# An attention kernel's eight-score phase: one exponential each for the first two scores, and a table of three phases for the PSUM banks

## The chip, the cores and the metric

The kernel runs on one core of one Trainium2 chip. The metric is the device time of one execution in microseconds (us). Beside the times there is a profile of one execution, in which the engines are called PE (TensorE, the matmuls), PEld (TensorE's loads of the stationary operand, called weight loads), ACT (ScalarE), DVE (VectorE), POOL (GpSimd) and SP (the engine that issues most DMAs). L829 means line 829 of the kernel.

## The reference

The output mixes two branches by a gate for each token: 32-head softmax attention, and an MLP over the token axis. All arrays are float32.

```python
x = A_x                                        # (1, 2048, 512)
g = sigmoid((x * gate_w).sum(-1, keepdims=True))
# a: full attention, H = 32 heads of Dh = 16, S = 2048 tokens
q, k, v = split_heads(x @ wqkv)
p = softmax(einsum("bhqd,bhkd->bhqk", q, k) * Dh ** -0.5)
a = merge_heads(einsum("bhqk,bhkd->bhqd", p, v)) @ wo
# b: token-mixing MLP, F = 1792
h = layernorm(x)
u = gelu(einsum("bsd,sf->bdf", h, w1) + b1)
b = transpose(einsum("bdf,fs->bds", u, w2) + b2)
out = g * a + (1 - g) * b
```

## The kernel before, in words

The kernel first makes v, then q and k (split in a high and a low float32r part and written to DRAM), then the first layer of the MLP. From about 305 us on it runs the attention, with the MLP's second layer and the output projection laid beside it on TensorE. The change lies in that part alone.

**Groups and phases.** There are 32 groups (`grp`): a pair of heads by half of the queries. A group has 8 phases, so there are 256 phases in all. A phase makes eight scores, s0 to s7 here: each is one matmul of 64 rows of contraction, 128 keys by 512 queries, written to a PSUM bank of its own (`score`, L829). The other 64 rows of the array are given to a matmul of the dense work (`dn`, L895), which is issued right behind a score and runs beside it. Most phases have six dense matmuls: then s0 and s1 run beside each other, on the two halves of the rows, and s2 to s7 have a dense one each. In the phases with eight dense matmuls every score has one. The table of the dense work (`put`, L672, with its sizes at L694, L696, L700, L706 and L707) gives eight to the first pair of phases, to nine pairs in the second layer's tiles 4, 8 and 12 and to the last eight pairs, that is to 36 of the 256 phases.

**Banks.** Of PSUM's eight banks one (`dn`) belongs to the dense work, and seven form `banks` (RING = 7). The table `TURN` says for each phase, in turn, which banks the eight scores take, and which bank v's products take. It has four rows, and four more that mirror them, so it repeats after eight phases.

**Exponentials.** ScalarE reads the scores and writes the exponentials into a tile `pt` with room for two scores. `exponentials` (L844) issues one instruction for two banks that lie side by side (128x1024) as soon as both scores are issued. In three of four rows a phase has four such instructions, called e0 to e3 here. In the third row the last two scores lie in banks 6 and 0, and e3 is two instructions of one bank each (128x512), which share one `pt`. The pool `ptp` has six buffers (L539), so e2 of a phase writes into the buffer that e0 of the phase before has filled.

**v's products.** After the scores of a phase TensorE multiplies v with the exponentials of the phase before (`apply_v`, L775, its matmul at L789). In the trace that is 32 matmul records in each phase, in four pairs of scores: the first pair reads s0 and s1 of the phase before, and so releases e0's `pt`. The products go to one bank, `av_bank`, and VectorE adds them to the group's sum (L809).

**What sets the order.** The order of each engine's instructions is written out by hand (`tc.manual_schedule`). TensorE's in one phase is: s0 to s7 with the dense matmuls, then v's products. `reads` and `writes` put a wait for each use of a bank: a score waits for what last read its bank.

In a phase two uses of banks come around within the phase itself: s7 takes a bank that s0 or s1 had, and v's products take the other of the two (row one: `3, 4, 5, 6, 0, 1, 2, 3`, v's products in 4). The other scores take banks from the phase before: s4 and s5 those of its e3, s6 the one that its v's products had and VectorE has read.

The POOL `token` (L899) orders the two halves of the dense rows, which add to one bank from phase to phase. `slow` holds VectorE's larger steps (reciprocals of the softmax sums, the scaling and splitting of attention output that `fetch_o` has brought from DRAM, L607 to L620), at most one for each phase, put ahead of the phase's addition.

Of the kernel before, what the change touches and what calls it, by code (L numbers as in the profile page):

```python
# [10 lines left out]
F32 = mybir.dt.float32  # L11
# [3 lines left out]
AF = mybir.ActivationFunctionType  # L15
# [7 lines left out]
P = 128  # L23
# [8 lines left out]
NB = 512  # L32
NQ = S // NB
VC = DH + 1
SCALE = DH**-0.5
# [24 lines left out]
def gated_mix(ctx: ExitStack, tc: tile.TileContext, a_x, a_wqkv, a_wo, b_w1, b_b1, b_w2, b_b2, gate_w, out):  # L60
    nc = tc.nc
# [353 lines left out]
    with tc.tile_pool(name="ln1", bufs=3, side="right") as ln, tc.tile_pool(name="gl", bufs=2, side="right") as gl:  # L415
# [22 lines left out]
        beside = {mybir.EngineType.Activation, mybir.EngineType.DVE, mybir.EngineType.Pool}  # L438
# [6 lines left out]
        for f0, cs in order.items():  # L445
            n = min(NB, F - f0) // P
# [65 lines left out]
    def second_out(t, ps):  # L512
# [13 lines left out]


    TURN = [
# [4 lines left out]
    ]  # L533
    TURN += [(tuple(RING - 1 - s for s in scores), RING - 1 - b) for scores, b in TURN]

    o_d = [[dram.tile([P, QW], F32, name=f"o{h}{k}") for k in range(ND)] for h in range(2)]
    r_d = [[dram.tile([P // DH, QW], F32, name=f"r{h}{k}") for k in range(ND)] for h in range(2)]
# [183 lines left out]
    def reads(ins, *at):  # L721
        for before in recent:
            if before.ins.engine != ins.ins.engine:
                tc.declare_no_dep(ins.ins, before.ins, reason="another bank")
        recent.append(ins)
        for bank in at:
            readers[bank].append(ins)
            for mm in writers[bank].values():
                tc.add_manual_dep(ins.ins, mm.ins.name, SYNC, reason="the bank is written")
# [45 lines left out]
    def apply_v(late, bank, end=False):  # L775

        if not late:
            return
        g, units = late
        pairs = [sorted(units[n : n + 2], key=lambda u: u[2]) for n in range(0, N_S, 2)]  # L780
        av = banks[:, bank, :]
        taken = [0, 0]

        for pair in pairs:
            for i, c, qb, pt, act in pair:
                taken[qb] += 1
                for h in range(2):
                    j = 2 * qb + h
                    mm = nc.tensor.matmul(  # L789
                        av[32 * j : 32 * j + VC, i * QC : (i + 1) * QC],  # L790
                        v[:, c, g % NP * 2 + i, :],
                        pt[:, h * QC : (h + 1) * QC],
                        start=taken[qb] == 1,
                        stop=taken[qb] == len(pairs),
                    )
                    writes(mm, bank, j, act)

        there = {(i, qb) for i, _, qb, *_ in units}
        if len(there) == 4:
            parts = list(zip(column_halves(sums[g]), column_halves(av))) if end else [(sums[g], av)]  # L800
        else:
            parts = []
            for i in sorted(range(2), key=lambda i: -sum(k[0] == i for k in there)):
                qbs = [qb for qb in range(2) if (i, qb) in there]
                if qbs:
                    at = slice(64 * qbs[0], 64 * (qbs[-1] + 1)), slice(i * QC, (i + 1) * QC)
                    parts.append((sums[g][at], av[at]))
        for x, y in parts:
            reads(nc.vector.tensor_tensor(x, y, x, ALU.add), bank)  # L809

    engines = {getattr(mybir.EngineType, name) for name in ("PE", "Activation", "DVE", "Pool", "SP")}
    with tc.manual_schedule(engines=engines):
        kt, qt = {0: load_k(0)}, {0: load_q(0)}
        late, fence = None, None

        for n, (step, *args) in enumerate(first):
            if n and n % 12 == 0:
                split_weight(nc.vector.tensor_copy, nc.vector.tensor_tensor)
            ps, a, b, start, stop, done = step(*args)
            nc.tensor.matmul(ps, a, b, start=start, stop=stop)  # L820
            if done:
                done()

        def score(grp, i, n, turn, units):

            c, qb = n // 2, (n + i) % 2
            bank = turn[len(units)]
            rows = slice(i * HALF, i * HALF + ROWS)
            mm = nc.tensor.matmul(  # L829
                banks[:, bank, :],  # L830
                kt[grp][rows, c * P : (c + 1) * P],
                qt[grp][rows, qb * NB : (qb + 1) * NB],
                start=True,
                stop=True,
            )
            writes(mm, bank)
            units.append([i, c, qb, None, None])
            beside = [m for m, unit in enumerate(units) if unit[3] is None and abs(turn[m] - bank) == 1]
            if beside:
                exponentials(turn, units, [sorted((beside[0], len(units) - 1), key=lambda m: turn[m])])  # L840
            elif len(units) == N_S:
                exponentials(turn, units, [[m] for m, unit in enumerate(units) if unit[3] is None])

        def exponentials(turn, units, runs):  # L844
            pt = ptp.tile([P, 2, NB], F32, name="pt")
            n = 0
            for run in runs:
                at = [turn[m] for m in run]
                dst = pt[:, n : n + len(at), :]
                act = nc.scalar.activation(dst, banks[:, at[0] : at[-1] + 1, :], AF.Exp, scale=SCALE)  # L850
                reads(act, *at)
                for m in run:
                    units[m][3:] = pt[:, n, :], act
                    n += 1

        for grp in range(NG):
            at = [0, 0]
            for ph in range(2 * TWOS):
                if ph == 0:
                    sums[grp] = out_pool.tile([P, NB], F32, name="ot")  # L860
                    nc.gpsimd.memset(sums[grp], 0.0)
                if ph == 0 and grp + 1 < NG:
                    qt[grp + 1] = load_q(grp + 1)
                if ph == 1 and grp + 1 < NG:
                    kt[grp + 1] = load_k(grp + 1)
                two, second = divmod(ph, 2)
                two += grp * TWOS
                if not second:
                    for what, *args in calls.get(two, ()):
                        what(*args)  # L870
                    beside = [step(*args) for step, *args in dense.get(two, ())]
                last_ph = grp == NG - 1 and ph == 2 * TWOS - 1
                if last_ph:

                    nc.vector.tensor_scalar_max(sums[grp], sums[grp], least[0])
                while stores:
                    stores.pop()()
                splits = bool(second and loaded and len(ready) < 2)
                ends = second and any(done for *_, done in beside)
                if not splits and (grp >= NG - TWOS or not ends):  # L880
                    for n, (ready_at, step) in enumerate(slow):
                        if ready_at <= two:
                            slow.pop(n)[1]()
                            break
                units = []
                turn, av_bank = TURN[(2 * two + second) % len(TURN)]
                for n in range(N_S - len(beside)):
                    i = (n + second + 1) % 2
                    score(grp, i, at[i], turn, units)
                    at[i] += 1  # L890
                half = slice(0, HALF) if second else slice(HALF, P)
                for m, (ps, a, b, first, last, done) in enumerate(beside):
                    score(grp, second, at[second], turn, units)
                    at[second] += 1
                    mm = nc.tensor.matmul(ps, a[half], b[half], start=first and not second, stop=last and bool(second))  # L895
                    if m == 0 and fence is not None:
                        tc.add_manual_dep(mm.ins, fence.ins.name, SYNC, reason=REASON)
                    if m == len(beside) - 1:
                        fence = nc.gpsimd.memset(token, 0.0)  # L899
                        tc.add_manual_dep(fence.ins, mm.ins.name, SYNC, reason=REASON)  # L900
                    if done and second:
                        done()
                if splits:
                    split_weight(nc.vector.tensor_copy)
                if grp == ph == 0:
                    shift_rows(nc.vector, k_bufs[1])
                apply_v(late, av_bank)
                if grp and not ph:
                    store_sums(grp - 1)
                late = grp, units  # L910
        assert not slow and not stores
        last_ot = sums[NG - 1]
        apply_v(late, TURN[0][1], end=True)
    psum_ctx.close()

    ptp_ctx.close()
# [161 lines left out]
```

## Time and profile before

| what | value |
|---|---|
| median of 3 runs | 1393.16 us (1390.81 to 1393.76) |
| the profiled execution, its own time | 1389.72 us |
| its span in the profile | 1387.9 us |
| granted TensorE clock, mean | 0.996 |
| busy share: PE / PEld / DVE / ACT / POOL | 99% / 56% / 43% / 79% / 15% |
| exponentials (L850) | 1088 instructions, first start 304.7 us, last start 1368.0 us |
| DMA | 136.86 MB, mean 99 GB/s |

The profiled execution lies 3.4 us under the median, within 0.3% of it. A matmul's end is modelled in the profile and matmuls overlap, so PE's 99% doesn't say that it has no room. In a row of the timeline stand the start, the length, the engine, the line, the operation with its output and inputs, the count of merged instructions, and in brackets the idle time of the engine before it with what the profile takes for its end.

### The profile page before, as it was taken

How to read it: one execution, taken by the hardware profiler on the slowest of the kernel's cores; microseconds unless marked ns; L12 is line 12 of the kernel's file. 1: busy time of each engine (PE TensorE's matmuls, PEld its weight loads, DVE VectorE, ACT ScalarE, POOL GpSimd, SP SyncE). 2: the span in 40 equal slices, each digit the busy share in tenths (PEclk: the TensorE clock that was granted, in tenths of full speed). 3: DMA queues.
4: the chain of work that ended last, by engine and by line, in shares of the span. 5: the costliest groups of instructions: out<-in, count | busy, mean ns of one | idle time of the engine just before them, and what ended most of it. 6: DMA issues, size and time to landing. Idle time of an engine off the chain costs nothing.

```text
span 1387.9 us, 32932 instructions
## 1 busy us (share of the span) xinstructions
PE 1371.2 (99%) x13282; PEld 776.8 (56%) x13282; DVE 592.8 (43%) x1040; ACT 1100.2 (79%) x1312; POOL 207.3 (15%) x435
## 2 busy tenths in 40 slices
PE   9999999999999999999999999999999999999998
PEld 7888888874444454444444454444454444444454
DVE  5675463183443333334434333333434333536424
ACT  3453343269999999999899999999999999998794
POOL 0210344551101011011010011101111011000000
PEclk9999999999999999999999999999999999999999
DMA  4596633273343233334434333333333333355511
GB/s 129 162 323 236 220 97 94 77 154 78 70 82 77 55 74 62 63 67 100 88 86 104 89 63 67 76 60 76 65 77 69 63 74 85 82 118 135 138 43 69
DMA packets 92524, 136.86 MB, mean 99 GB/s; under 512 B 14197, under 2 KB 53259, under 8 KB 89292
## 3 DMA queue, kind: packets, MB, share of 16 engines
q1 hardware_dynamic: 91788, 133.63, 40.3%
q8 instruction: 106, 1.74, 0.5%
q10 hardware_dynamic: 576, 1.05, 0.2%
q14 instruction: 54, 0.44, 0.1%
HBM read 98.85 MB, written 35.78 MB: 97 GB/s over the span
## 4 chain that ended last, share of the span: by engine, by line
PE 94%; DMA 3%; SPq 1%; DVE 1%; ACT 0%; issue 0%; DVEq 0%
PE s L789 33%; PE s L829 32%; PE acc L413 11%; PE acc L74 9%; PE dn L895 8%; DMA o_sum<-r 2%; PE pa L934 1%; PE acc L185 0%; SPq L499 0%; PE acc L252 0%; DMA x<-in_A_x_dram 0%; DMA qs<-qp 0%; DMA ks<-kp 0%; DVE o_sum L619 0%; ACT pt L850 0%; PE pa L964 0%
## 5 line engine op out<-in xcount | busy, mean ns | idle before, releaser
L850 ACT ACTIVATE pt<-s 128x1024 f32<-128x1024 f32 (+1 forms) x1088 | 972.2, 981 | 92.9 <-PE s L789 71.5
L829 PE MATMUL s<-qs,ks 64*128 64x512 f32 x2048 | 598.3, 441 | 6.4 <-DVE ot L809 5.0
L789 PE MATMUL s<-pt,v 128*17 128x256 f32 x8192 | 492.9, 381 | 0.0
L829 PEld LDWEIGHTS s<-qs,ks 64*128 64x128 f32 x2048 | 300.8, 184 | 317.3 <-ACT pt L850 292.8
L809 DVE TENSOR_TENSOR ot<-s,ot 128x256 f32<-128x256 f32 x476 | 202.8, 426 | 573.2 <-PE s L789 530.1
L789 PEld LDWEIGHTS s<-pt,v 128*17 128x17 f32 x8192 | 215.5, 97 | 214.5 <-issue 64.2
L895 PE MATMUL dn<-u_hi,w_lo 64*128 64x512 f32 x430 | 206.5, 480 | 0.0
L895 PE MATMUL dn<-u_lo,w_hi 64*128 64x512 f32 x430 | 171.2, 398 | 0.0
L895 PE MATMUL dn<-u_hi,w_hi 64*128 64x512 f32 x428 | 170.2, 398 | 0.0
L67 POOL TENSOR_TENSOR w_lo<-w_raw,w_hi 128x512 fp32r<-128x512 f32 (+1 forms) x126 | 149.4, 1187 | 125.6 <-ACT w_hi L66 107.3
L899 POOL MEMSET token<- 1x1 f32 x256 | 22.8, 89 | 936.5 <-PE dn L895 936.5
L765 DVE RECIPROCAL rt<-rt 128x256 f32<-128x256 f32 x62 | 108.7, 1753 | 2.1
L66 ACT CAST w_hi<-w_raw 128x512 fp32r<-128x512 f32 (+1 forms) x67 | 38.1, 569 | 79.4 <-PE acc L413 58.8
L413 PE MATMUL acc<-h_hi,w_hi 128*128 128x512 f32 x224 | 87.1, 389 | 0.0
L413 PE MATMUL acc<-h_lo,w_hi 128*128 128x512 f32 x224 | 87.1, 389 | 0.0
L413 PE MATMUL acc<-h_hi,w_lo 128*128 128x512 f32 x224 | 87.1, 389 | 0.0
L895 PEld LDWEIGHTS dn<-u_lo,w_hi 64*128 64x128 f32 x430 | 79.3, 184 | 7.7
L895 PEld LDWEIGHTS dn<-u_hi,w_hi 64*128 64x128 f32 x428 | 79.5, 186 | 0.3
L895 PEld LDWEIGHTS dn<-u_hi,w_lo 64*128 64x128 f32 x430 | 78.7, 183 | 0.2
L74 PE MATMUL acc<-xt_hi,wc_hi 128*128 128x512 f32 x128 | 49.8, 389 | 0.0
L74 PE MATMUL acc<-xt_lo,wc_hi 128*128 128x512 f32 x128 | 49.8, 389 | 0.0
L74 PE MATMUL acc<-xt_hi,wc_lo 128*128 128x512 f32 x128 | 49.8, 389 | 0.0
(142 smaller groups left out, 1001.1 us busy)
## 6 DMA issues: line engine op xcount, KB each, us to landing
w_raw<-in_B_w_dram SPq DMA_DIRECT2D x96, 256.0 KB
ks<-kp SPq DMA_DIRECT2D x192, 128.0 KB
qs<-qp SPq DMA_DIRECT2D x256, 64.0 KB
qp<-pc SPq DMA_DIRECT2D x16, 768.0 KB
x<-in_A_x_dram SPq DMA_DIRECT2D x32, 256.0 KB
kp<-pc SPq DMA_DIRECT2D x16, 512.0 KB
w_raw<-in_B_w_dram SPq DMA_DIRECT2D x32, 128.0 KB
bp<-row SPq DMA_DIRECT2D x16, 256.0 KB
```

The lines of the kernel that those rows point to most:

```text
L66: copy(hi, src)
L67: return sub(lo, src, hi.bitcast(F32), ALU.subtract)
L74: nc.tensor.matmul(ps, a, b, start=start and n == 0, stop=stop and n == last)
L413: nc.tensor.matmul(p, a, b, start=first and k == 0, stop=last and k == 2)
L765: nc.vector.reciprocal(rt[0][:, cols], rt[0][:, cols])
L789: mm = nc.tensor.matmul(av[32 * j : 32 * j + VC, i * QC : (i + 1) * QC], v[:, c, g % NP * 2 + i, :], pt[:, h * QC : (h + 1) * QC], start=t ...
L809: reads(nc.vector.tensor_tensor(x, y, x, ALU.add), bank)
L829: mm = nc.tensor.matmul(banks[:, bank, :], kt[grp][rows, c * P : (c + 1) * P], qt[grp][rows, qb * NB : (qb + 1) * NB], start=True, stop=True,)
L850: act = nc.scalar.activation(dst, banks[:, at[0] : at[-1] + 1, :], AF.Exp, scale=SCALE)
L895: mm = nc.tensor.matmul(ps, a[half], b[half], start=first and not second, stop=last and bool(second))
L899: fence = nc.gpsimd.memset(token, 0.0)
L934: nc.tensor.matmul(pa[t], a, b, start=i == 0 and t not in LATE, stop=i == len(mms) - 1 and t in LATE)
```

## The change

Each row of the table now also names the exponentials. In every phase s0 and s1 get an exponential of one bank each, which share one `pt`; the other six scores get three of two banks. s7 takes the bank of s0, and v's products take the bank of s1, in every row. The table has three rows, without mirrored ones. In the third row the pairs are s2 with s4, s5 with s6, and s3 with s7. A phase has five exponentials and four `pt` tiles in every row; before it was four exponentials in three rows of four, and five in the fourth, and also four `pt` tiles. The last v's products take the bank of the row that follows. TensorE's matmuls, their order, VectorE's work, the `pt` pool's six buffers and all DMAs stay as they are.

```diff
     TURN = [
-        ((3, 4, 5, 6, 0, 1, 2, 3), 4),
-        ((5, 6, 0, 1, 2, 3, 4, 5), 6),
-        ((0, 1, 2, 3, 4, 5, 6, 0), 1),
-        ((4, 5, 2, 3, 0, 6, 1, 5), 4),
+        ((3, 4, 5, 6, 0, 1, 2, 3), ((0,), (1,), (2, 3), (4, 5), (6, 7)), 4),
+        ((5, 6, 0, 1, 2, 3, 4, 5), ((0,), (1,), (2, 3), (4, 5), (6, 7)), 6),
+        ((0, 2, 3, 1, 4, 5, 6, 0), ((0,), (1,), (2, 4), (5, 6), (3, 7)), 2),
     ]
-    TURN += [(tuple(RING - 1 - s for s in scores), RING - 1 - b) for scores, b in TURN]
...
-        def score(grp, i, n, turn, units):
+        pt = None
+
+        def score(grp, i, n, turn, exps, units):
...
             units.append([i, c, qb, None, None])
-            beside = [m for m, unit in enumerate(units) if unit[3] is None and abs(turn[m] - bank) == 1]
-            if beside:
-                exponentials(turn, units, [sorted((beside[0], len(units) - 1), key=lambda m: turn[m])])
-            elif len(units) == N_S:
-                exponentials(turn, units, [[m] for m, unit in enumerate(units) if unit[3] is None])
-
-        def exponentials(turn, units, runs):
-            pt = ptp.tile([P, 2, NB], F32, name="pt")
-            n = 0
-            for run in runs:
-                at = [turn[m] for m in run]
-                dst = pt[:, n : n + len(at), :]
-                act = nc.scalar.activation(dst, banks[:, at[0] : at[-1] + 1, :], AF.Exp, scale=SCALE)
-                reads(act, *at)
-                for m in run:
-                    units[m][3:] = pt[:, n, :], act
-                    n += 1
+            for which in exps:
+                if which[-1] == len(units) - 1:
+                    exponential(turn, units, which)
+
+        def exponential(turn, units, which):
+            nonlocal pt
+            if which[0] != 1:
+                pt = ptp.tile([P, 2, NB], F32, name="pt")
+            which = sorted(which, key=lambda m: turn[m])
+            first, at = which == [1], [turn[m] for m in which]
+            dst = pt[:, first : first + len(at), :]
+            act = nc.scalar.activation(dst, banks[:, at[0] : at[-1] + 1, :], AF.Exp, scale=SCALE)
+            reads(act, *at)
+            for n, m in enumerate(which):
+                units[m][3:] = dst[:, n, :], act
...
-                turn, av_bank = TURN[(2 * two + second) % len(TURN)]
+                turn, exps, av_bank = TURN[(2 * two + second) % len(TURN)]
...
-        apply_v(late, TURN[0][1], end=True)
+        apply_v(late, TURN[(2 * two + second + 1) % len(TURN)][-1], end=True)
```

More of the change, by code (lines that the diff above doesn't have):

```diff
@@ L885, in gated_mix @@
                 units = []
-                turn, av_bank = TURN[(2 * two + second) % len(TURN)]
+                turn, exps, av_bank = TURN[(2 * two + second) % len(TURN)]
                 for n in range(N_S - len(beside)):
                     i = (n + second + 1) % 2
-                    score(grp, i, at[i], turn, units)
+                    score(grp, i, at[i], turn, exps, units)
                     at[i] += 1
@@ L892, in gated_mix @@
                 for m, (ps, a, b, first, last, done) in enumerate(beside):
-                    score(grp, second, at[second], turn, units)
+                    score(grp, second, at[second], turn, exps, units)
                     at[second] += 1
```

## The prediction

> **What bounds the kernel now.** First the page and the groups by form, for the size of the stage; then the waits, for who stands still in it; then the timeline of a single phase, for the ring of waits that sets its length.
>
> ```profile
> span 1387.9 us, 32932 instructions
> PE 1371.2 (99%) x13282; PEld 776.8 (56%) x13282; DVE 592.8 (43%) x1040; ACT 1100.2 (79%) x1312; POOL 207.3 (15%) x435
> ```
> ```profile
> L850 ACT ACTIVATE pt<-s x1088: 592/1024/1072, 304.7 to 1368.0; 128x1024 f32<-128x1024 f32 x161, 128x512 f32<-128x512 f32 x21
> ```
> ```profile
> PEld s L829 <- ACT pt L850: 292.8, 737, 0.6
> ACT pt L850 <- PE s L789: 71.5, 199, 4.3
> PEld s L789 <- issue: 64.2, 260, 0.7
> ```
>
> The attention runs from 304.7 to 1368 us, 1063 us for 256 phases, or 4.15 us each. The waits show a ring: scores wait for exponentials (737 times), and exponentials for v's products (199 times). Neither engine is full: each waits for the other in every phase. So PE's 99% is not the bound. A phase in the timeline:
>
> ```profile
> 707.22 3.77 ACT L850 ACTIVATE pt<-s 128x1024 f32<-128x1024 f32 x4 [0.31 <-PE s L789]
> 711.32 3.84 ACT L850 ACTIVATE pt<-s 128x1024 f32<-128x1024 f32 x5 [0.32 <-PE s L789]
> 715.46 1.02 ACT L850 ACTIVATE pt<-s 128x1024 f32<-128x1024 f32 x1 [0.31 <-ACT pt L850]
> ```
> ```profile
> 708.14 1.02 ACT L850 ACTIVATE pt<-s 128x1024 f32<-128x1024 f32 x1
> 709.05 1.95 ACT L850 ACTIVATE pt<-s 128x1024 f32<-128x1024 f32 x2
> 712.24 1.08 ACT L850 ACTIVATE pt<-s 128x512 f32<-128x512 f32 x2
> 712.72 1.52 ACT L850 ACTIVATE pt<-s 128x512 f32<-128x512 f32 x2
> 713.19 1.05 ACT L850 ACTIVATE pt<-s 128x1024 f32<-128x1024 f32 x1
> ```
> ```profile
> 708.32 0.18 PEld L829 LDWEIGHTS s<-qs,ks 64*128 64x128 f32 x2 [0.42 <-ACT pt L850]
> ...
> 708.51 0.88 DVE L809 TENSOR_TENSOR ot<-s,ot 128x256 f32<-128x256 f32 x2 [1.09 <-PE s L789]
> ...
> 709.22 0.18 PEld L829 LDWEIGHTS s<-qs,ks 64*128 64x128 f32 x1 [0.37 <-ACT pt L850]
> ...
> 709.56 0.39 PE L829 MATMUL s<-qs,ks 64*128 64x512 f32 x1
> ...
> 709.56 0.18 PEld L829 LDWEIGHTS s<-qs,ks 64*128 64x128 f32 x1
> ...
> 709.79 0.39 PE L829 MATMUL s<-qs,ks 64*128 64x512 f32 x1
> ...
> 710.13 0.18 PEld L829 LDWEIGHTS s<-qs,ks 64*128 64x128 f32 x1 [0.39 <-ACT pt L850]
> ```
> ```profile
> 710.56 1.43 PEld L789 LDWEIGHTS s<-pt,v 128*17 128x17 f32 x32 [0.24 <-issue]
> 712.42 0.18 PEld L829 LDWEIGHTS s<-qs,ks 64*128 64x128 f32 x2 [0.42 <-ACT pt L850]
> ```
>
> A run of exponentials begins with the one that waits for v's products, so it is e2 (its `pt` was e0's, which the first pair of v's products frees). The run is e2, e3, then e0, e1 of the next phase; the two singles at 712.24 and 712.72, right behind an e2, are the e3 of row three and confirm the numbering. 708.32 is the load for s0 and s1, 709.22 for s4, the matmul at 709.79 is s6, the load at 710.13 is s7's, and 710.56 starts v's products. The ring that closes the phase, start to start:
>
> - e2 to e3, 707.22 to 708.14: 0.92. e3 to e0, 708.14 to 709.05: 0.91.
> - e0's start to s7's load, 709.05 to 710.13: 1.08. s7 takes a bank that e0 reads.
> - s7's load to v's products, 710.13 to 710.56: 0.43.
> - v's products to the next e2, 710.56 to 711.32: 0.76, the first pair's work.
>
> The sum is 4.10, the distance from 707.22 to 711.32. In row three e3 is two singles, 0.95 in place of 0.91, and the distance from 711.32 to 715.46 is 4.14. With three such phases in four the mean is 4.11.
>
> ```profile
> 1304.44 3.85 ACT L850 ACTIVATE pt<-s 128x1024 f32<-128x1024 f32 x4 [0.33 <-PE s L789]
> 1308.61 3.85 ACT L850 ACTIVATE pt<-s 128x1024 f32<-128x1024 f32 x4 [0.33 <-PE s L789]
> ```
>
> In the 36 phases with eight dense matmuls it is 4.17, since e0 must wait for an s1 that comes one matmul later.
>
> **The change, part by part.** *e0 split in two.* Two singles start 0.48 apart (712.24 to 712.72, 712.72 to 713.19), and the last of them ends 0.60 after its start (712.24 + 1.08 = 713.32). ScalarE gets 0.96 of work where it had 0.91, in 192 phases more: 192 x 0.05 = 10 us of ScalarE's time. It lies beside ScalarE's idle 0.31 per phase, and would cost 10 us if that cover were gone.
>
> *s7 waits for the first single only.* It can load at e0's start + 0.60 + 0.06 = 0.66, where it had 1.08; the 0.06 is the signal's way, as from e3's end (708.14 + 1.02) to s4's load (709.22). The 0.43 that follows stays.
>
> *v's products get a new wait*, for the second single: e0's start + 0.48 + 0.60 + 0.06 = 1.14, against 0.66 + 0.43 = 1.09 by way of s7. The stall moved there would be 0.05. Queued behind v's products are the next s0 and all of TensorE's phase, and e2 waits for their first pair.
>
> *What is late next.* With only these waits the ring would be 0.92 + 0.91 + 1.14 + 0.76 = 3.73. Another ring is longer. s4 still waits for e3, in all three new rows (banks 0, 2 and 4 are e3's of the row before), and TensorE issues in order:
>
> - e2 to e3: 0.92. e3 to s4's load, 708.14 to 709.22: 1.08. Both stay.
> - s4's load to the next score's matmul, 709.22 to 709.56: 0.34. This is 0.11 more than the 0.23 from 709.56 to 709.79, because a load that has waited hides behind nothing.
> - s5 to s6 and s6 to s7: 0.23 each. s7 no longer waits: it could load at e2 + 0.92 + 0.91 + 0.66 = 2.49, and its turn comes at 0.92 + 1.08 + 0.34 + 0.23 = 2.57.
> - s7's matmul to v's products: 0.43 less the 0.11 of a waiting load, 0.32. They begin at e2 + 3.12, by when the second single (2.97) is done.
> - v's products to e2: 0.76.
>
> Sum: 0.92 + 1.08 + 0.34 + 0.23 + 0.23 + 0.32 + 0.76 = 3.88. ScalarE's own work is 0.92 + 0.91 + 0.48 + 0.48 + 0.91 = 3.70, so 0.18 of its wait is left. TensorE's own is 1.86 for v's products up to the next s0 (710.56 to 712.42), 0.11 for its exposed load, 6 x 0.23 to s7, and 0.32: 3.67. With eight dense matmuls a seventh step makes it 3.90, above the ring. Both edits are shorter there.
>
> *VectorE.* Its addition ends at 708.51 + 0.88 = 709.39 and s6's load stands at 709.56; its turn comes with s5's matmul at 709.56. The offset from v's products to s6 doesn't change, but what lateness VectorE had was hidden by s7's wait, and now has 0.1 us of room. I take nothing for it and leave it for the range.
>
> *The table.* In the third row s1 takes a bank of the e2 before, free at e2 + 1.02 + 0.06 = 1.08; its turn comes at 712.42 - 711.32 = 1.10. The pairing of s2 with s4 and s3 with s7 delays e1 and e3 only to matmuls that lie before their turns (s4's ends near e2 + 2.5, e1 starts at 2.79). In the phase behind it e3 waits for the third pair of v's products, two quarters of their 1.86 behind the first, which is level with e3's turn at 0.92. Nothing is added for these. The mirrored rows had other bank numbers and the same waits.
>
> *Stalls with another cause.*
>
> ```profile
> DVE o_sum L619 <- DMA o_sum<-r: 16.0, 4, 5.5
> ```
> ```profile
> L619 DVE TENSOR_TENSOR o_sum<-o_lo,o_sum x8: 1210/1226/1227, 658.1 to 1360.3; 128x1024 f32<-128x1024 f32 x7, 96x1024 f32<-96x1024 f32 x1
> ```
> ```profile
> 1283.16 0.62 SPq L617 DMA_DIRECT2D o_sum<-r  x1
> ...
> 1290.10 1.23 DVE L619 TENSOR_TENSOR o_sum<-o_lo,o_sum 128x1024 f32<-128x1024 f32 x1 [4.80 <-DMA o_sum<-r]
> ```
>
> Four of the eight scalings waited for a transfer, up to 5.5 us, with the addition queued behind. The transfer took 6.9 us from its issue to its use (1283.16 to 1290.10), and a shorter phase brings the use sooner by two times 0.23. That is 0.46 for each of the four. Between nothing and 8 us (all eight exposed, by 1 us each) I take 3 us, since others come near; and some five phases that such waits stretch gain nothing: 1 us.
>
> **The sum.** 220 phases gain 4.11 - 3.88 = 0.23: 50.6. 36 gain 4.17 - 3.90 = 0.27: 9.7. Less 4: 56 us. The profiled execution's own time is 1389.7, so 1333 for its like. It lies 3.4 under the median of the runs; on the median, 1393.2 - 56 = 1337 us.
>
> The Trainium skill ("ScalarE: Activation LUTs", section "What ACT_TABLE_LOAD costs") gives each such instruction a fixed 186 ns beside 0.833 ns per element, with an overlap of some 93 ns from one to the next; an estimate from it is 0.946 for a pair, 0.520 for a single and 3.88 of ScalarE work in a phase. That speaks against splitting, since ScalarE itself would then be as long as the new ring and no shorter phase could follow. The rows above (0.91 and 0.48) leave 0.18 more, and go into the sum.
>
> **The rivals.** *A deeper gain.* If s4's wait for e3 cost less than it does now, only ScalarE's work or the ring of 3.73 would be left: 220 x 0.38 + 10 - 4 = 90 us, 1303. Against it stands s4's wait of 0.37 in the phase shown, of which all three rows keep the cause. By the Trainium skill's figures it has no room at all. 0.04.
>
> *Half of the gain given back.* s6 behind a late VectorE, v's products behind the second single, or more exposed transfers: 0.1 us a phase, 220 x 0.1 = 22, and so 1359 us; up to 1385 for 0.22. For it: the new margins are 0.08 for s7, 0.15 for v's products, about 0.1 for s6. Against it: in the phase shown DVE had idled 1.09 before its addition. 0.12.
>
> *Slower.* One mechanism: the second single doesn't follow at once. If it started as late after the first as a pair does (0.91, for instance because an access to the neighbouring bank holds it), v's products would begin at e0 + 0.91 + 0.66 = 1.57, the ring would be 0.92 + 0.91 + 1.57 + 0.76 = 4.16, or 0.05 over 4.11 in 220 phases: 11 us, 1404. It decides from a distance of 0.86 on (4.11 - 0.92 - 0.91 - 0.76 - 0.66). Against it: 0.48 in the rows of before. 0.04.
>
> *The change doesn't do what it says*: s7 held by the second single, as it is by the pair now. Then s7 loads at e0 + 1.14, v's products follow at 1.57, and the ring is 4.16 as well, 1404 us. Against it: each of the two is an instruction of its own with a signal of its own. 0.02.
>
> **How the numbers follow.** A measurement of this kernel can tell about 0.2%, 2.8 us, from no change. The forecast, 1337 us, has 0.78; its own range, for a phase between 3.83 and 3.94 and transfers between 0 and 8 us, is 1324 to 1354. The range given reaches a little into the second rival, to 1358, and down to 1322. Faster by over 0.2%: 0.78 + 0.04 + 0.12 = 0.94, less 0.01 for the far end of the second rival: 0.93; within 0.2%: 0.01; slower: 0.04 + 0.02 = 0.06.
>
> **What would show it.** Right: runs of exponentials from e2 to e2 at 3.88 apart in every row, five in each; before e2 an idle time of about 0.2 in place of 0.31; before s4 still a wait for ACT; before s7 and before v's products none. Wrong: distances of 3.7 (deeper gain), a wait of s6 for VectorE's addition or of v's products for ACT (given back), or singles more than 0.5 apart (slower). The whole forecast falls if s4's wait goes or if a new one appears between s4 and e2.

## The result, and the profile after

The changed kernel takes 1336.75 us (median of 4 runs, 1336.19 to 1337.52) against 1392.45 us before (median of 4). The ratio is 0.9601, with a 95% interval from 0.9584 to 0.9618: 55.7 us less. The profiled execution took 1337.52 us, with a span of 1335.7; its span is 52.2 us shorter than that of before. Of the four executions of the second experiment below, one was a slow one of 2502.35 us, which is in the median given there, but not in the ratio.

The head of the page, and the exponentials in the groups by form, first before the change (L850) and then after it (in the changed kernel L849; v's products are L787, the dense matmuls L893, VectorE's addition L807):

```profile
span 1335.7 us, 32958 instructions
PE 1313.7 (98%) x13282; PEld 780.3 (58%) x13282; DVE 592.7 (44%) x1040; ACT 1110.4 (83%) x1504; POOL 206.7 (15%) x435
```
```profile
L850 ACT ACTIVATE pt<-s 128x1024 f32<-128x1024 f32 x960 | 917.3, 1031 | 92.9 <-PE s L789 71.5 <-ACT pt L850 17.5 <-PE s L829 4.0
```
```profile
L849 ACT ACTIVATE pt<-s 128x1024 f32<-128x1024 f32 x768 | 767.1, 1033 | 27.7 <-issue 11.6 <-PE s L829 4.0 <-PE s L787 3.1
...
L849 ACT ACTIVATE pt<-s 128x512 f32<-128x512 f32 x512 | 280.1, 610 | 2.7 <-PE s L829 2.6
```

ScalarE has 192 exponentials more and 10 us more work (1110.4 against 1100.2), and still the time fell. Its idle time ahead of the exponentials fell from 92.9 us to 27.7 + 2.7. The waits (engine and line, whom it waited for, us in all, times, longest):

```profile
PEld s L829 <- ACT pt L849: 185.8, 471, 0.8
...
PEld s L787 <- ACT pt L849: 91.1, 250, 0.4
...
ACT pt L849 <- PE s L787: 3.1, 3, 2.1
```

Scores wait 471 times for an exponential where it was 737, and exponentials for v's products three times where it was 199. One phase in the timeline, the exponentials first (each row is the view of a short stretch, so it begins where the single instruction does, and its length may take in the next one), then the weight loads, and s7's matmul:

```profile
693.96 1.94 ACT L849 ACTIVATE pt<-s 128x1024 f32<-128x1024 f32 x2
694.88 1.51 ACT L849 ACTIVATE pt<-s 128x1024 f32<-128x1024 f32 x2
695.78 1.09 ACT L849 ACTIVATE pt<-s 128x512 f32<-128x512 f32 x2
696.26 1.53 ACT L849 ACTIVATE pt<-s 128x512 f32<-128x512 f32 x2
697.82 1.02 ACT L849 ACTIVATE pt<-s 128x1024 f32<-128x1024 f32 x1
```
```profile
693.21 1.43 PEld L787 LDWEIGHTS s<-pt,v 128*17 128x17 f32 x32 [0.36 <-ACT pt L849]
695.06 0.19 PEld L829 LDWEIGHTS s<-qs,ks 64*128 64x128 f32 x2 [0.42 <-ACT pt L849]
...
695.95 0.18 PEld L829 LDWEIGHTS s<-qs,ks 64*128 64x128 f32 x1 [0.35 <-ACT pt L849]
...
696.29 0.18 PEld L829 LDWEIGHTS s<-qs,ks 64*128 64x128 f32 x1
...
696.53 0.18 PEld L829 LDWEIGHTS s<-qs,ks 64*128 64x128 f32 x1
...
697.08 0.13 PEld L787 LDWEIGHTS s<-pt,v 128*17 128x17 f32 x8 [0.36 <-ACT pt L849]
```
```profile
696.75 0.39 PE L829 MATMUL s<-qs,ks 64*128 64x512 f32 x1
```

693.96 is e2, 694.88 e3, 695.78 and 696.26 the two singles, 697.82 the next e2: 3.86 us later. s4 still waits for e3 (695.95 is 1.07 behind 694.88). s7's load at 696.53 waits for nothing: the first single began 0.75 before and lasts 0.6. From v's products at 693.21 to the next at 697.08 it is 3.87.

One label misleads. The profile puts 0.36 of idle time ahead of v's products down to ACT, 250 times. But the second single (696.26, some 0.6 long) ends about 0.2 before 697.08. What comes 0.32 before 697.08 is s7's matmul (696.75), 0.23 behind s6's. Before the change it was 0.43 from s7's load, of which 0.11 was the load that had waited, so the same 0.32, and then v's products had no wait for ACT to come. So it is s7's matmul that holds them, and the label is the last event that the profile saw.

Phase by phase, from the first weight load of v's products to the next, and apart from a few long ones (5 before, 10 after): before, 4.08 to 4.10 and behind row three 4.15 to 4.16; after, 3.86 to 3.87 in all three rows. With eight dense matmuls: before 4.17 to 4.20, after 3.89 to 3.92.

### The profile page after: what moved, and what is told of

Read it like the earlier page. It is cut to its first block, busy times and chain, and to the rows that moved or that the text cites. A ratio compares the mean times of both kernels' runs of the same rounds, so it can differ in the third digit from the quotient of the medians.

```text
span 1335.7 us, 32958 instructions
## 1 busy us (share of the span) xinstructions
PE 1313.7 (98%) x13282; PEld 780.3 (58%) x13282; DVE 592.7 (44%) x1040; ACT 1110.4 (83%) x1504; POOL 206.7 (15%) x435
## 3 DMA queue, kind: packets, MB, share of 16 engines
q10 hardware_dynamic: 576, 1.05, 0.2%
## 4 chain that ended last, share of the span: by engine, by line
PE 94%; DMA 3%; DVE 1%; SPq 1%; ACT 0%; issue 0%; DVEq 0%
PE s L787 34%; PE s L829 29%; PE acc L413 11%; PE acc L74 9%; PE dn L893 7%; DMA o_sum<-r 2%; PE pa L932 1%; PE acc L185 1%; PE acc L252 0%; PE dn L818 0%; SPq L499 0%; DVE o_sum L617 0%; DVE ot L807 0%; ACT pt L849 0%; PE acc L229 0%; DMA row<-part 0%
## 5 line engine op out<-in xcount | busy, mean ns | idle before, releaser
L849 ACT ACTIVATE pt<-s 128x1024 f32<-128x1024 f32 (+1 forms) x1280 | 982.5, 864 | 30.4 <-issue 11.6
L829 PE MATMUL s<-qs,ks 64*128 64x512 f32 x2048 | 537.0, 429 | 10.6 <-DVE ot L807 9.8
L787 PE MATMUL s<-pt,v 128*17 128x256 f32 x8192 | 496.3, 383 | 0.0
L807 DVE TENSOR_TENSOR ot<-s,ot 128x256 f32<-128x256 f32 x476 | 202.7, 426 | 524.2 <-PE s L787 480.5
L787 PEld LDWEIGHTS s<-pt,v 128*17 128x17 f32 x8192 | 216.4, 98 | 246.3 <-ACT pt L849 91.1
L893 PE MATMUL dn<-u_hi,w_lo 64*128 64x512 f32 x430 | 187.2, 435 | 0.0
L893 PE MATMUL dn<-u_lo,w_hi 64*128 64x512 f32 x430 | 169.6, 394 | 0.0
L893 PE MATMUL dn<-u_hi,w_hi 64*128 64x512 f32 x428 | 169.2, 395 | 0.0
L897 POOL MEMSET token<- 1x1 f32 x256 | 22.6, 88 | 884.5 <-PE dn L893 884.5
L893 PEld LDWEIGHTS dn<-u_lo,w_hi 64*128 64x128 f32 x430 | 79.4, 185 | 6.8
L893 PEld LDWEIGHTS dn<-u_hi,w_hi 64*128 64x128 f32 x428 | 79.7, 186 | 0.3
L893 PEld LDWEIGHTS dn<-u_hi,w_lo 64*128 64x128 f32 x430 | 79.0, 184 | 0.4
L893 PE MATMUL dn<-wo_hi,o_hi 64*128 64x512 f32 x112 | 46.3, 413 | 4.3 <-DVE row L635 4.3
```

What stands on the lines that cost most here:

```text
L787: mm = nc.tensor.matmul(av[32 * j : 32 * j + VC, i * QC : (i + 1) * QC], v[:, c, g % NP * 2 + i, :], pt[:, h * QC : (h + 1) * QC], start=t ...
L829: mm = nc.tensor.matmul(banks[:, bank, :], kt[grp][rows, c * P : (c + 1) * P], qt[grp][rows, qb * NB : (qb + 1) * NB], start=True, stop=True,)
```

## The experiments

All were compared with the kernel before on the same chip; "ratio" is to its time, with a 95% interval. "Phase" is again the distance of v's products, and "long phases" is what the few phases lie above the median phase by more than 0.15 us, added up: 11.1 us before the change, 22.6 us after it.

**s0's and s1's banks swapped.** Only the table differs:

```diff
-        ((3, 4, 5, 6, 0, 1, 2, 3), ...
-        ((5, 6, 0, 1, 2, 3, 4, 5), ...
-        ((0, 2, 3, 1, 4, 5, 6, 0), ...
+        ((4, 3, 5, 6, 0, 1, 2, 3), ...
+        ((6, 5, 0, 1, 2, 3, 4, 5), ...
+        ((2, 0, 3, 1, 4, 5, 6, 0), ...
```

> The changed kernel with the banks of s0 and s1 swapped in every row, so that s7 waits for the second single and v's products for the first. Nothing else changes. Theory (the gain comes from s7's bank being free after one single): the ring is e2 to e3 0.92, to the first single 0.91, to s7 0.48 + 0.62 + 0.05 = 1.15, to v's products 0.43, to e2 0.76, sum 4.17 in every row, against 3.86 measured with the change; the time goes to some 1400 to 1411 us, 0.5 to 1.3% above the kernel before. Rival (the gain comes from the table of three rows or from the split as such, whichever single frees which bank): 3.86 again, 1337 us.

Measured: 1399.94 us, ratio 1.0042 (1.0025 to 1.0059). The exponentials from e2 on, and the weight loads of s7 and of v's products:

```profile
703.85 3.84 ACT L849 ACTIVATE pt<-s 128x1024 f32<-128x1024 f32 x5 [0.31 <-ACT pt L849]
708.00 3.84 ACT L849 ACTIVATE pt<-s 128x1024 f32<-128x1024 f32 x5 [0.31 <-ACT pt L849]
```
```profile
706.82 0.18 PEld L829 LDWEIGHTS s<-qs,ks 64*128 64x128 f32 x1 [0.45 <-ACT pt L849]
...
707.25 1.43 PEld L787 LDWEIGHTS s<-pt,v 128*17 128x17 f32 x32 [0.24 <-issue]
```

The phase is 4.15, s7 waits again, and ScalarE's 0.31 before e2 is back. So the whole gain hangs on s7's bank being the first single's: with the same singles and the same three rows, the other order is slightly slower than the kernel before, by 0.4%.

**One exponential for s0 and s1 again, in two rows of three.**

```diff
-        ((3, 4, 5, 6, 0, 1, 2, 3), ((0,), (1,), (2, 3), (4, 5), (6, 7)), 4),
-        ((5, 6, 0, 1, 2, 3, 4, 5), ((0,), (1,), (2, 3), (4, 5), (6, 7)), 6),
+        ((3, 4, 5, 6, 0, 1, 2, 3), ((0, 1), (2, 3), (4, 5), (6, 7)), 4),
+        ((5, 6, 0, 1, 2, 3, 4, 5), ((0, 1), (2, 3), (4, 5), (6, 7)), 6),
```

> The changed kernel with one exponential of two banks for s0 and s1 in rows one and two, as before the change; row three keeps its two singles. Theory: a phase's length goes by its own row: 4.10 in rows one and two, 3.86 in row three, seen one by one in the trace; mean 4.02, the time some 1370 to 1378 us. Rival (the table makes the gain): 3.86 in all rows, 1337 us. Rival (the split acts across phases): one length in all rows, somewhere between.

Measured: 1374.60 us, ratio 0.9844 (0.9824 to 0.9863). The loads of v's products:

```profile
705.71 1.43 PEld L787 LDWEIGHTS s<-pt,v 128*17 128x17 f32 x32 [0.36 <-ACT pt L849]
709.80 1.43 PEld L787 LDWEIGHTS s<-pt,v 128*17 128x17 f32 x32 [0.25 <-issue]
713.88 1.43 PEld L787 LDWEIGHTS s<-pt,v 128*17 128x17 f32 x32 [0.25 <-issue]
717.75 0.34 PEld L787 LDWEIGHTS s<-pt,v 128*17 128x17 f32 x11 [0.36 <-ACT pt L849]
```

4.09, 4.08 and 3.87: each phase has the length of its own row.

**The eight rows of before, with the two singles.**

```diff
+        ((3, 4, 5, 6, 0, 1, 2, 3), ((0,), (1,), (2, 3), (4, 5), (6, 7)), 4),
+        ((5, 6, 0, 1, 2, 3, 4, 5), ((0,), (1,), (2, 3), (4, 5), (6, 7)), 6),
+        ((0, 1, 2, 3, 4, 5, 6, 0), ((0,), (1,), (2, 3), (4, 5), (6, 7)), 1),
+        ((4, 5, 2, 3, 0, 6, 1, 5), ((0,), (1,), (2, 3), (4, 6), (5, 7)), 4),
     ]
+    TURN += [(tuple(RING - 1 - s for s in scores), exps, RING - 1 - b) for scores, exps, b in TURN]
```

(A pair whose banks don't lie side by side, s6 and s7 of row three, is issued as two singles.)

> The table of before, with its eight rows, and with the two singles for s0 and s1; e3 stays a pair where its banks lie side by side, and two singles in row three. Theory (it is which single frees s7's bank that counts): in rows one to three s7 has s0's bank, 3.86; in row four s7 has s1's and v's products s0's, as in e1_swap, and e3 ahead of it is two singles: 4.15 + 0.05 = 4.19. Mean 3.94, which makes 1350 to 1358 us. Rival (the table of three rows makes the gain): 4.1 in all rows, 1393 us or more. Rival (the split alone makes it): 3.86 in all rows, 1337 us.

Measured: 1358.33 us, ratio 0.9744 (0.9726 to 0.9763).

```profile
703.99 1.43 PEld L789 LDWEIGHTS s<-pt,v 128*17 128x17 f32 x32 [0.25 <-issue]
707.86 1.43 PEld L789 LDWEIGHTS s<-pt,v 128*17 128x17 f32 x32 [0.36 <-ACT pt L853]
711.73 1.43 PEld L789 LDWEIGHTS s<-pt,v 128*17 128x17 f32 x32 [0.37 <-ACT pt L853]
715.59 1.43 PEld L789 LDWEIGHTS s<-pt,v 128*17 128x17 f32 x32 [0.36 <-ACT pt L853]
719.79 1.43 PEld L789 LDWEIGHTS s<-pt,v 128*17 128x17 f32 x32 [0.24 <-issue]
```

3.87, 3.87, 3.86 and, in row four, 4.20. So the split makes the gain, in the old table too; what the table of three rows adds is that no row has the other order, nor an e3 of two singles ahead of it, which together is worth 1358.33 less 1336.75, about 22 us.

**e3 split as well.** In the loop over a row's exponentials, with `(0,)` and `(1,)` as they are:

```diff
-        ((3, 4, 5, 6, 0, 1, 2, 3), ...
+        ((3, 4, 5, 6, 1, 0, 2, 3), ...
...
-                    exponential(turn, units, which)
+                    for part in [which] if which[-1] < N_S - 1 else [which[:1], which[1:]]:
+                        exponential(turn, units, part)
...
-            if which[0] != 1:
+            if which[0] not in (1, N_S - 1):
```

> The changed kernel with e3 split in two singles as well, the one that frees s4's bank first (in row one s4 and s5 swap banks for it). Theory (the ring is now closed by s4's wait for e3): s4 is free 0.4 earlier, that ring falls to 3.71, and ScalarE's own work of 0.92 + 4 x 0.48 + 0.91 = 3.75 is the bound; phases with eight dense matmuls stay at 3.90. Gain 0.11 x 220 = 24 us, less some 3 for longer waits on transfers: 1313 to 1319 us, s4's waits for ACT nearly gone, ScalarE idle under 0.05 per phase. Rival (s4's wait is only late beside another bound, TensorE or VectorE's addition): 3.86 or a little more, 1337 to 1340 us. Rival (the next wait is s6's for VectorE's addition, with 0.1 of room): 3.78 to 3.85, 1318 to 1335 us, with waits of L829 for DVE.

Measured: 1323.36 us, ratio 0.9487 (0.9471 to 0.9503). The phase is 3.79, not 3.75, and the long phases come to 26.6 us, 4 more. The weight loads of s4, s5, s7 and v's products, and the second single of s0 and s1:

```profile
693.90 0.18 PEld L829 LDWEIGHTS s<-qs,ks 64*128 64x128 f32 x1
...
694.28 0.18 PEld L829 LDWEIGHTS s<-qs,ks 64*128 64x128 f32 x1 [0.20 <-ACT pt L850]
...
694.77 0.18 PEld L829 LDWEIGHTS s<-qs,ks 64*128 64x128 f32 x1
...
695.26 1.43 PEld L787 LDWEIGHTS s<-pt,v 128*17 128x17 f32 x32 [0.30 <-ACT pt L850]
...
699.06 1.00 PEld L787 LDWEIGHTS s<-pt,v 128*17 128x17 f32 x24 [0.30 <-ACT pt L850]
```
```profile
694.57 0.64 ACT L850 ACTIVATE pt<-s 128x512 f32<-128x512 f32 x1
```

s4's wait is gone, which shows that it closed the changed kernel's ring. (s5 at 694.28 now waits for the second half of e3, but v's products don't hang on that.) What holds v's products is the second single of s0 and s1: 694.57 + 0.64 + 0.05 = 695.26, while s7's matmul, at 694.86, is 0.40 before them and not 0.32. That ring was 3.73 in the prediction, and the added single lengthens it by 0.05 to 3.78. The expectation had forgotten that. It was not ScalarE's own work that bound: e2 starts 0.97 behind e1, where 0.91 would do.

**The scaling of the attention output one pair of phases later**, for seven of its eight parts:

```diff
-        slow.append((two + 1, lambda: nc.vector.tensor_mul(rb, raw, rb)))
-        slow.append((two + 1, lambda: split(hi, lo, rb, nc.vector.tensor_copy, nc.vector.tensor_tensor)))
+        at = two + (2 if pairs == 4 else 1)
+        slow.append((at, lambda: nc.vector.tensor_mul(rb, raw, rb)))
+        slow.append((at, lambda: split(hi, lo, rb, nc.vector.tensor_copy, nc.vector.tensor_tensor)))
```

> The changed kernel with the scaling of the attention output (seven of the eight) due one pair of phases later behind its transfers. Theory: in the changed kernel's trace nine phases are together some 22 us longer than their neighbours, against 11 us before the change, because the scaling stands in VectorE's queue ahead of the addition that s6 waits for, and waits there for a transfer of fixed length; with some 7.7 us more for the transfer most of this goes: 1317 to 1324 us, and VectorE's idle time ahead of the scaling falls from above 20 us to under 5. Rival (the transfers start late because of the queue, and would be late all the same): 1333 to 1337 us.

Measured: 1328.82 us, ratio 0.9531 (0.9515 to 0.9547). The long phases fall from 22.6 to 13.7 us, of which 8.6 stand in one phase and have a new cause. In the DMA queue and on VectorE there:

```profile
1219.34 0.43 SPq L614 DMA_DIRECT2D o_lo<-o  x1
1226.77 0.62 SPq L615 DMA_DIRECT2D o_sum<-r  x1
1227.43 0.46 SPq L632 DMA_DIRECT2D row<-part  x1
```
```profile
1225.52 1.23 DVE L67 TENSOR_TENSOR o_lo<-o_sum,o_hi 128x1024 fp32r<-128x1024 f32 x1
1234.45 0.75 DVE L636 SCALAR_TENSOR_TENSOR row<-dn,g,row 128x512 f32<-128x512 f32 x1 [7.71 <-DMA row<-part]
```

The later scaling holds the only `o_sum` buffer longer. The next transfer into it waits in SP's queue until the last reader of the buffer is done (1225.52 + 1.23 = 1226.75; nothing was issued since 1219.34), and the `row` that an output needs stands right behind it. Theory and rival were each half right: VectorE's idle time ahead of the eight scalings fell from 22 to 3 us, as the theory had it, but the time fell by only 7.9, since a new wait came up in the queue.

**Both, and two `o_sum` buffers in the second half** (`bufs=1 + half` in `fetch_o`):

> The changed kernel with three edits: e3 split as in e3_split_last, the scalings due one pair of phases later as in e4_later, and two buffers instead of one for the second half's o_sum, so that its transfer doesn't wait in SP's queue for the scaling before. Theory: phases of 3.79 as in e3_split_last (the ring over the second single of s0 and s1: 0.92 + 3 x 0.48 + 0.69 + 0.76), which is 0.07 x 220 = 15 us below the changed kernel, and of its 22 us of long phases some 4 left: 1300 to 1308 us. Rival (the row that waits in SP's queue in e4_later waits for the transfers themselves, not for the buffer): one phase stays 8 us long, 1309 to 1316 us.

Measured: 1305.42 us, ratio 0.9367 (0.9347 to 0.9388). The long phases come to 5.0 us. Of the waits for this transfer one is left:

```profile
DVE o_sum L618 <- DMA o_sum<-r: 2.7, 1, 2.7
```

It is the fastest of all, 31 us below the changed kernel.

**VectorE's addition made late**, in the changed kernel and in the kernel before (the added instruction stands only in the 220 phases in which the addition has two parts):

```diff
-        for x, y in parts:
+        for n, (x, y) in enumerate(parts):
+            if n == 1:
+                nc.vector.tensor_tensor(parts[0][0], parts[0][0], parts[0][0], ALU.max)
             reads(nc.vector.tensor_tensor(x, y, x, ALU.add), bank)
```

> The changed kernel with one more VectorE instruction between the two parts of the addition of v's products (the greater of a part of the sum and itself, 128x256, which changes nothing in it), some 0.43 us, so that s6's bank is free that much later. Theory (the change used up VectorE's room): s6's load at 0.43 + 2.99 behind the start of v's products, s7 and the next v's products right behind it: 3.42 + 0.11 + 0.23 + 0.32 = 4.08 in place of 3.86, 1375 to 1392 us, with waits of L829 for DVE in every phase. Rival (VectorE still has half a microsecond of room): 1337 to 1342 us.

> The kernel before the change with the same additional VectorE instruction. Theory (before, s7's wait for e0 hid a late VectorE): s6 can come 0.4 later and s7 still waits for e0, 4.10 as it was, 1391 to 1397 us. Rival (s6 binds here too): 0.2 more for each phase, 1430 to 1450 us.

Measured: in the changed kernel 1390.28 us (ratio 0.9983, 0.9973 to 0.9993), 53.5 us more than without it; in the kernel before 1398.82 us (1.0036, 1.0025 to 1.0047), 5.6 us more. The added instruction takes 0.425 us. The changed kernel's v's products, s6 and v's products:

```profile
546.02 1.43 PEld L787 LDWEIGHTS s<-pt,v 128*17 128x17 f32 x32 [0.37 <-issue]
...
549.45 0.18 PEld L831 LDWEIGHTS s<-qs,ks 64*128 64x128 f32 x1 [0.39 <-DVE ot L809]
...
550.12 1.43 PEld L787 LDWEIGHTS s<-pt,v 128*17 128x17 f32 x32 [0.37 <-ACT pt L851]
```

And s6, s7 and v's products in the kernel before:

```profile
548.03 0.18 PEld L831 LDWEIGHTS s<-qs,ks 64*128 64x128 f32 x1 [0.33 <-DVE ot L811]
...
548.31 0.18 PEld L831 LDWEIGHTS s<-qs,ks 64*128 64x128 f32 x1
...
548.74 1.43 PEld L789 LDWEIGHTS s<-pt,v 128*17 128x17 f32 x32 [0.24 <-issue]
```

s6 waits for VectorE in both, 0.39 and 0.33. In the changed kernel that goes into the phase (4.11 in place of 3.86): of 0.43 us of lateness 0.25 come through, so that some 0.18 of room was left (the prediction had about 0.1). In the kernel before the phase stays at 4.08 to 4.12 (4.15 to 4.16 behind row three), as s7 waits for e0 anyway: e0 starts at 547.22, lasts 1.05, and s7's load at 548.31 is 0.05 behind its end. What grew there are the long phases, from 11.1 to 19.2 us; that is most of the 9.6 us between the spans of the two profiles, and the profile of before lies under its median. So the change did use up most of VectorE's room.

## Why the prediction was right

The median came out at 1336.75 for a forecast of 1337, and by the mechanism that was forecast. The closeness is partly luck: the regular phases gained 3.4 us more than the sum had and the stalls cost 7.5 more, and the 4 us that this leaves are made up by where the two profiled executions happen to lie beside their medians (both below).

- *The ring of before, 4.10*: shown. Swapping which single frees s7's bank gives back 4.15; a pair in a row gives 4.08 to 4.09 in that row alone.
- *s7 no longer waits*: shown by the changed kernel's rows.
- *What is late next, s4 behind e3, 3.88*: 3.86 measured, and term by term, from e2 to e3, s4's load, the matmuls of s5, s6 and s7, v's products and the next e2: 0.92, 1.07, 0.34, 0.24, 0.23, 0.32 and 0.74. The split of e3 removed s4's wait and the phase fell to 3.79. So it was the closing wait, and the rival of a deeper gain without touching it was rightly put low.
- *v's products behind the second single*: the new wait cost nothing, as forecast, though the profile's label says otherwise 250 times. It does bind once e3 is split.
- *Singles 0.48 apart*: 695.78 to 696.26. The Trainium skill ("ScalarE: Activation LUTs", section "What ACT_TABLE_LOAD costs") has instructions back to back overlap by some 93 ns; by an estimate from it, a phase with e3 split too (two pairs, four singles) needs 2 x 0.946 + 4 x 0.520 = 3.97 of ScalarE. That phase measured 3.79, and in the rows above the distances are 0.48 and 0.91 where the estimate has 0.520 and 0.946, so the measurement decides against the page here. The rows of before were the right price.
- *ScalarE's idle time before e2*, about 0.2: e2 starts 0.18 later than e1 would let it, but the profile shows next to none (27.7 us in all), since it counts from the end of an exponential that lasts 1.03 on average, not from the 0.91 after which the next one could start. The sign named in the prediction was put on the wrong base.
- *The sum.* The profile's span fell by 52.2 us. The long phases grew by 22.6 - 11.1 = 11.5 us. So the regular phases gave 52.2 + 11.5 = 63.7 us, against 50.6 + 9.7 = 60.3 in the sum: 3.86 in place of 3.88.
- *Stalls with another cause*, put at 3 + 1 us: this is the term that was mis-sized. It measured 11.5 us, above the bound of 8. The step that failed is that a shorter phase brings the use sooner by 0.46 for each of the four transfers, and that nothing else moves. VectorE's four exposed waits were 16.0 us before (4.43, 1.24, 5.54 and 4.80) and 22.0 after (5.99, 3.17, 7.22 and 5.61). The longest of them in SP's queue and on VectorE, before and then after:

```profile
1239.13 0.63 SPq L617 DMA_DIRECT2D o_sum<-r  x1
...
1249.56 1.23 DVE L619 TENSOR_TENSOR o_sum<-o_lo,o_sum 128x1024 f32<-128x1024 f32 x1 [5.54 <-DMA o_sum<-r]
```
```profile
1189.40 0.63 SPq L615 DMA_DIRECT2D o_sum<-r  x1
...
1199.99 1.23 DVE L617 TENSOR_TENSOR o_sum<-o_lo,o_sum 128x1024 f32<-128x1024 f32 x1 [7.22 <-DMA o_sum<-r]
1201.25 0.88 DVE L807 TENSOR_TENSOR ot<-s,ot 128x256 f32<-128x256 f32 x2
1202.16 0.69 DVE L66 CAST o_hi<-o_sum 128x1024 fp32r<-128x1024 f32 x1
1202.89 1.23 DVE L67 TENSOR_TENSOR o_lo<-o_sum,o_hi 128x1024 fp32r<-128x1024 f32 x1
```

This wait grew by 1.7. From the issue to the use it took 10.43 us before and 10.59 after, nearly the same; but from the issue to VectorE standing ready (the use less the wait) it was 4.89 before and 3.37 after. So 1.5 of the 1.7 is that the issue comes later against VectorE's work. SP issues other transfers back to back for 13.0 us ahead of it (13.8 after), from 1226.17 and 1175.59 on, which is the same place of the same phase. From there VectorE is ready 0.67 sooner in the changed kernel, as its phases are shorter, and the issue comes 0.85 later, as SP's run of issues is not shorter but longer. The prediction had let the issue move with the phase.

Over all four, VectorE stands ready 3.0 us sooner behind the issue (0.28 to 1.52 each), and the transfers take 3.0 longer from issue to use (0.16 to 1.41 each). Why they take longer stays open; in the run with swapped banks, whose phases are not shorter than before the change, the same four were 1.9 longer, so part of it may be a difference between single executions.

And the wait has an echo: the cast and the subtraction (1.9 us) stand ahead of the next addition, which now has little room, so the phase behind was 2.2 us longer than a regular one in place of 0.7. Behind three of the four waits these phases cost 4.0 us more than before. The prediction named both halves, the queue and the lost room, but priced only the first. That a later use takes these stalls away is shown by the two experiments with the later scaling.

- *Profile and median.* The profile of before happened to lie 3.4 us under its median, that of after 0.8 us above, within the spread of single runs. Seen from the profiled execution alone the forecast was 1333, and 1337.5 came.

## What to carry to other kernels

When two engines wait for each other in a ring, add up the ring start to start, find the one hand-over that closes it, and split only the instruction that holds it: here a second instruction of 0.05 us of ScalarE's time per phase bought 0.25, and only if the half that is done first is the one that frees what is needed first. Then add up the next ring before building, and look for whoever lived in the slack that goes away: an engine that was late in hiding comes into the open. A wait's label in the profile names the last event seen; check it against the distances before believing it. And a transfer's issue does not move with a shorter loop when its queue has a run of other issues ahead of it.

## What the runs showed of the hardware that was not expected

An exponential of one bank lasts 0.60 to 0.64 us and one of two banks 1.02 to 1.08, yet they follow each other at 0.48 and at 0.91 to 0.92: neighbours overlap by 0.10 to 0.16 us, so that splitting a pair costs 0.05. The forecast had used these distances; not expected was that singles last longer the further they stand in a back-to-back run (0.60, 0.61, 0.62 and 0.64 for the four with e3 split as well), while their distance stays at 0.48. So the end of an exponential, and the idle time counted from it, don't tell when the next one could have started.
